# Batch 3's scaled q and k turned by transfers from SP, and joined copies in batch 0, in a gated-attention and mixer kernel

## The chip, the cores and the metric

The kernel runs on one core of a Trainium2 chip. The engines named here are TensorE (PE; its weight loads are listed as PEld), VectorE (DVE), ScalarE (ACT), GpSimd (POOL) and SyncE (SP, which only issues transfers). The metric is the device time of one execution in microseconds, as the median of several runs. A change of less than 1% can't be told from none.

## What is computed

```
f = 1 / (1 + exp(-f_logit))                          # (4, 8, 768, 48): batch, head, step, dim
state = f[t] * state + outer(k[t], v[t])             # per batch and head, 48 x 48
y[t] = q[t] @ state                                  # for 768 steps
x = y, heads side by side                            # (4, 768, 384)
h = relu(x^T @ w_tok1) @ w_tok2                      # mixing over steps, 768 -> 256 -> 768
u = x + h^T
out = u + relu(u @ w_ch1) @ w_ch2                    # mixing over channels, 384 -> 1536 -> 384
```

Inputs and output are float32.

## The kernel before, in words

The 768 steps of a batch are cut into 6 chunks of 128. Within a chunk the recurrence is written as a masked product: ACT makes the log of the gate (`exp`, then `ln`, lines 365 and 366), a cast splits it into a high and a low bf16 part (the low part is `Llo`, line 373), TensorE sums both over the steps with a triangular matrix (`sums`, lines 432 and 433), and ACT takes two exponentials of the sums, `G` and `Gi` (lines 442 and 444). DVE multiplies them onto q and k (`gated`, line 461). These scaled q and k are `qk`, 128 steps by 2 x 8 heads x 64 columns in bf16; 48 of the 64 columns of a head are data.

TensorE needs them with the steps along the columns. In `turn` (line 471) it makes eight transposes of 128 x 128 per chunk into one bank of PSUM, and DVE or ACT copies the bank, 128 x 1024, into `qkT` (`turned`, lines 343 and 345: helpers that serve many copies). Then follow the scores (line 384), the product of the last step's k with v for the state (`parts`, line 400), the mask on DVE (line 512), the new state (lines 520 to 525) and the results (lines 532 and 536). There are two buffers `qkT`, for even and odd chunks, so a chunk's turned q and k can be written when the results of two chunks before are done. From batch 1 on the totals of the gates go through a transfer of 2 KB from SP (`glast`).

Batch 0 goes by pairs of chunks (`pair`, lines 586 to 702): there the two chunks of a pair are dealt out by odd and even steps, so its turned q lies with the columns of both chunks interleaved (`qTp`), and its masks are the constants `pmask`, built by DVE from a triangle (`tri_bf`) and the identity. Turned q and k of each chunk go into banks of their own and are copied one by one (`turned`, four copies of 128 x 512 per pair); the same banks then take the scores.

The mixer of a batch (lines 711 to 809) has two products over the steps (`tok1` line 716, `tok2` line 732), a transpose of the sum (`ut`, line 764, copied into `uT`), and two products over the channels (`ch1` line 780, `ch2` line 798), after which DVE adds the input (line 804) and SP stores 128 rows (line 808).

All four batches overlap: attention of a batch runs between the mixer matmuls of the batch before. The order is not found by the engines but written out by hand in `ORDER`, a list of numbers of operations. Each token is an operation (its place in the order in which the code adds them); a letter behind it picks the engine (A for ACT, D for DVE, G for POOL), a number behind a colon the PSUM bank, and `z3` stands for three filler matmuls on a block of ones (line 826), which write to a bank that is not read. Every engine works through its own operations in the order of this list, SP too: a transfer whose data isn't ready holds back the ones behind it. The loads of q, k, v, gates and weights are issued by POOL, the first gates by SP. The code already holds a path in which a batch named in `TURNED` gets its scaled q and k turned by a transfer; before the change the tuple is empty.

```
if b in TURNED:
    add(("turn", b, c), SP, lambda: nc.sync.dma_start_transpose(
        out=qkT[it], in_=qk[i].rearrange("t n h d -> t (n h d)")), need=[("qh", i), ("kh", i)],
        make=[("qkT", it, 0), ("qkT", it, 1)], kind=("xfer", 1300, 3060))
    return [Bank(), Bank()]
```

Of the kernel before, what the change touches and what calls it, by code (L numbers as in the profile page):

```python
# [22 lines left out]
TURNED = ()  # L23
# [9 lines left out]
41 42 19 8 43 18 27 7 25 5 16 17 26 29 0 6 1 9 44 12 24 61 30 13 32 2 58 46 14 15 10 62 3 31 59 63D 45 64 35 28 33 67  # L33
34 60D 47 65 11 40 70 37 z14 123:0 48 66D 68 73 69D 50 114:1 71 125 72D 162:2 49 116 128 124 118 51 115 39 153:3 36 20
38 74 121:1 117 126 155 75G 127 135:0:4 164 119:5 141 154 131:6 53 157 129:0 120A 146 202:3 132D 130A 143G 167 156 163
52 134 165 122A 166 160:4 138 54 193:2 204 142A 139 161A 133 147 203 137 z1 174:6:0 148G 205 195 168:3 149G 136 194
158:1 76 169A 180 z1 140:5:2 196 159A 181 170:6 197 150 206 171A 172 187 151A 207 z1 173 175 183G 152A 198:0 182G 176
208:2 199A 56 210:1 209A 178 z1 200:4 211A 55 177 201A z3 213 188 77 145A 179:3:6 218 144A 212 217 184 236:5 228:1
185A 215 190G 237 186A 78 214:2 216 189A 238 229 191 220 219:4:3 192A 221 4 223A 222G z1 224 230 80 226 225D 231 239
227A 21 232 240 82 233 241 235D 234A 243A 242D 248:1 244:7 252:2 249 361 260 245 250 261 362 264 246 253 263A 265 363G  # L40
256 254 262A 257 247 266A 272:5 268:4 81 259A 258D 270:0 388:7 273A 269D 278:6 79 271D 391 274:5 279D 276:4 255 292:0
277A 57 267D 300:6 275A 370 294:4 301D 358 326:5 293D 359 302:6 23 371 322:0 327D 303A 324:3 367 360D 316:5 84 295A
251 306:6 389 325D 372G 368 310:1 307D 320:4 311D 83 380:3 308:2 382 87 318:1 383 309D 282:6 390 384 86 321A 284:2 392
381 312:4 369G 323A 385 314:3 285A 393 319A 296:0 91 364 304:2 297D 313A 394:1 305D 373 386:4 395A 283D 286:2 317D
280:0 365 290:5 374 281D 366G 298:6 287A 387D 315A 424:0 375G 22 291A 398:2 299A 396:3 401 397:5 426 409 403G 453:7
427 399 416:6 402G 288:2 428 85 407 418 333:4 419 400 88 456 338:1 408 289A 457 417 404:3 93 420 334 425 421 413:6 90
335 415A 89 405A 422:0 336 343:5 423A 429 92 461:4 406D 430:2 414D 95 462 344 455 431D 463 432:6 410 454 433:3 436
434:4 411A 412A 339 437 94 435 491:6 484:7 345 438 98 445 440A 439A 441:0 444 340 100 442A 458 485 450:2 446 101 464
353:3 452A 341 451A 97 459:4 447 443A 486 492 460A 465:2 448G 99 354 466D 449A 469:0 96 467:1 472 355 470 487 471
468:0 348:4 473 479 474A 475G 493 606 476:1 376 480 609 349 477D 607 494 346 481:0 488 495 482A 483D 350 610 608D 489  # L50
615 496 611G 624:0 490D 497A 328:5 356 612 105 498:6 478D 627 501:3 616 351 628 504:1 626 499 632:7 617G 625 329 505
634 502 510:0 613 506G 513:1 629 503A 500G 507:3 514 633 330 618 508 515G 518:6 635 637 520:4 516:1 614G 630:3 636
521D 517A 511 638:7 342 519A 106 331 668:1 631A 530:6 639D 108 660:0 531A 640:4 661 641:5 509G 644 642:6 663 512G
534:2 662 643 669 550:4 107 652 535A 522:3 538:0 621 523D 103 551A 526:5 524:3 548:2 856 527D 102 525D 532:5 651 857
542:3 670 104 539D 619 528:7 543D 533A 552:0 109 549D 671 540:3 622 620D 672 111 544:2 850 553D 664 572:1 673 851
574:0 645 573A 852G 566:5 665 529A 697:1 545A 646G 536:7 567A 112 700 576:2 537D 647A 701 110 575A 648:5 541D 546:7
332 649A 653 657:3 650D 623G 357 547A 558:6 659D 699 666:0 378 698 654 674:5 658D 655A 667A 554:7 675D 678:3 559A
677:1 681 676:4 656A 555D 858G 853 577 682 865 689 562:7 377 705:6 690 680 560:1 706 556:3 688 563A 581:4 854 702 684A
683G 578 707 855G 582 579 113 868:6 708 583 679 871 869 568:2 872 584 859 685:0 561D 866 585 703:5 870 352 694:7 704D
557A 709:1 696A 691 570:3 569A 710D 693G 695A 713:6 692G 711:2 716 686A 712:4 379 715 735:6 586:7 723 736 876:2 714  # L60
728:1 587 879 687D 860 564:5 724 878 861G 737 877 717 588 571D 718A 719A 720:2 565D 738 873 729 721A 596:3 862 881 730
722A 867D 725:4 597 589 726A 731 874:2 739 732 875A 598 740 727A 733 904:5 734D 741A 882:7 599 912:4 883A 754:1 757:3
755 745:6 907 748:0 758 915 591:1 746 914 759G 916 749 742:3 913 880 751:6 905 743 750G 580 885:0 906 884:4 337 756G
744A 895 886:3 747A 908 592 752 347 888 760:7 753A 601:6 761A 889 593 863 897 909 891A 864G 762:3 890A 764:7 917 602
765A 763D 896 768:4 766:7 792:3 594 767A 603 887 793A 769A 770:1 910:0 604 918:4 898 911A 901:6 900G 941:2 919D 902A
788:3 903A 771D 892:7 921:5 894D 893A 920:6 943 922:1 923 789A 800:7 933 899A 778:0 942 924 816:3 810:5 779D 776:6
801D 782:0 932 774:7 925 783A 946 780:4 777A 811D 772:0 944 781D 812:6 945 773A 926 605 808:2 775A 934 927G 796:0 817A
600 928G 813A 949:7 818:3 950 814:6 819A 802:5 951 806:3 952 784:7 809D 929:1 797D 785A 790:2 931D 815A 938:7 930A
791D 979:6 794:0 798:2 795D 953:1 803D 799A 786:0 939A 954D 947:5 787A 935 972:2 940A 980 948D 840:0 807A 937A 981
936A 957:3 956:7 960 955:4 967 825:3 958 973 820:1 959 982 974 961 835:5 968 962G 964:4 963G 975 826 966A 965A 969:7  # L70
827 970A 976 983 828 830:4 829 977 984 831 978A 985A 804:2 821 805A 832 822 998:2 823 989:6 845:3 990 986:1 999 991A
992:6 987 1000A 841 993 971A 988G 995:1 994A 836 996 1001:6 997G 1008:1 1004:7 1002 1006:2 842 833 1003A 1005D 837
1009A 1007D 846 1012:2 1014:1 847 1013A 1015D 1010:1 1030:7 1011A 1016:4 1031D 1018:6 1017D 1052:7 848 1019A 1044:4
1053D 849 1054:3 1028:7 1055D 1058:1 838 1056:3 1029D 839 1060:5 1059D 1057A 834 1026:7 1061A 590 1040:3 1027D 824
1062:1 1041A 1050:6 1045A 1020:5 1063A 1051D 1042:4 843 1046:6 844 1036:0 1047A 1032:1 1021A 1022:3 1043A 1048:5
1038:4 1094:6 1024:7 1039A 1023A 1079:2 1037A 1089:3 1049A 1033A 1069:4 1025A 1064:0 1034:1 1095 1084:5 1035D 1080
1085 1090 1074:1 1096 1081 1097 1098 1091 595 1086 1070 1087 1065 1082 1092 1075 1093 1071 1088 1076 1083 1072 1066
1073 1077 1078 1067 1068
"""


# [65 lines left out]
def kernel(  # L147
# [147 lines left out]
    for b, c in sorted(TOTALS):  # L295
        memset(f"L{b}{c}", L[b % 2][:, c, :, D:64], 0.0, [("L", b % 2, c)], 200)
# [7 lines left out]
    for i in range(len(state_bd)):  # L304
        memset(f"sbd{i}", state_bd[i], 0.0, [("sbd", i)], 220)
# [553 lines left out]
```

## Time and profile before

| | us |
|---|---|
| median of 3 runs | 177.97 (177.92 to 179.67) |
| the profiled execution | 178.3 |
| its span, first to last instruction | 176.6 |
| TensorE busy | 167.6 (95%) |
| DVE, ACT, POOL busy | 127.9, 120.2, 82.4 |

The profile is of one execution. It lists busy time by engine and the span in 40 slices; windows give the busy time of each engine in a stretch that is chosen (PE, PEld, DVE, ACT, POOL, each with its count, then the granted clock of TensorE, the share of the DMA engines and GB/s). The chain of waits goes back from the last instruction, at each step to what released it, and is shown in order of time (start, length, what). The groups list instructions of one kind with their busy time, the mean in ns of one, and the idle time before them with what ended it. The transfers are listed with their size and the time from issue to landing. Matmuls are pipelined, so the duration listed for one is longer than what it adds to a row of them; a row's length divided by its count gives the latter.

### The profile page before, as it was taken

The numbers are of one execution on the slowest core, as the hardware profiler recorded it, in microseconds if no ns is written. First come the engines' busy times: TensorE is split into PE (matmuls) and PEld (weight loads), VectorE is DVE, ScalarE is ACT, GpSimd is POOL, SyncE is SP. The second block draws the span as 40 slices with busy tenths as digits, with TensorE's granted clock in tenths as the row PEclk, the third lists the DMA queues.
The fourth block names the chain that finished last, engine by engine and source line by source line (L and its number), as shares of the span: only waits on it lengthen the run. The fifth ranks groups of instructions, "written<-read, shape, count | busy, mean of one in ns | idle before, by whom it ended". The sixth has DMA issues, their size and how long they took to land.

```text
span 176.6 us, 4600 instructions
## 1 busy us (share of the span) xinstructions
PE 167.6 (95%) x1835; PEld 107.7 (61%) x1838; DVE 127.9 (72%) x294; ACT 120.2 (68%) x273; POOL 82.4 (47%) x106
## 2 busy tenths in 40 slices
PE   6999898999999999999999999999999999999991
PEld 2466674556676665765757576676676566566660
DVE  6699987986879789897888968989476174830142
ACT  3999967869987569999969679775772444265000
POOL 4977946691799958998993503200001010000000
PEclk9999999999999999999999999999999999999999
DMA  5999999999599998999999991200200100150034
GB/s 149 226 171 184 227 218 206 148 197 156 34 87 138 205 130 179 142 117 91 137 135 149 156 77 47 89 4 0 91 4 0 48 0 0 74 193 4 0 135 176
DMA packets 78500, 19.98 MB, mean 113 GB/s; under 512 B 71216, under 2 KB 77664, under 8 KB 78480
## 3 DMA queue, kind: packets, MB, share of 16 engines
q0 software_dynamic: 69600, 13.77, 89.5%
q1 hardware_dynamic: 8880, 5.93, 11.0%
q8 instruction: 14, 0.23, 0.6%
q14 instruction: 6, 0.05, 0.1%
HBM read 25.17 MB, written 4.72 MB: 169 GB/s over the span
## 4 chain that ended last, share of the span: by engine, by line
PE 65%; DVE 11%; DMA 8%; ACT 7%; POOL 3%; issue 3%; DVEq 0%; POOLq 0%; ACTq 0%
PE ps L780 23%; PE ps L798 19%; DMA f_sb<-in_f_logit_dram 8%; PE ps L732 4%; PE ps L716 3%; PE ps L471 3%; ACT f_sb L365 2%; POOL qk_sb L265 2%; DVE Llo L373 2%; PE ps L764 2%; PE ps L384 1%; PE ps L612 1%; PE ps L433 1%; PE ps L432 1%; PE ps L536 1%
## 5 line engine op out<-in xcount | busy, mean ns | idle before, releaser
L798 PE MATMUL ps<-w_ch,zT 128*128 128x384 bf16 (+2 forms) x300 | 54.9, 320 | 0.0
L780 PE MATMUL ps<-uT,w_ch 128*128 128x384 bf16 x288 | 51.7, 326 | 0.6 <-DVE uT L345 0.3
L780 PEld LDWEIGHTS <-w_ch 128*128 128x128 bf16 x288 | 27.4, 97 | 18.1 <-issue 1.2
L798 PEld LDWEIGHTS <-zT 128*128 128x128 bf16 x300 | 27.4, 97 | 16.6 <-issue 0.4
L351 ACT ACTIVATE zT<-ps 128x384 bf16<-128x384 f32 x56 | 25.1, 496 | 11.2 <-PE ps L780 11.0
L353 DVE TENSOR_SCALAR zT<-ps 128x384 bf16<-128x384 f32 x40 | 20.9, 552 | 12.3 <-PE ps L780 12.2
L512 DVE TENSOR_TENSOR AmT<-ps,tri_bf 128x512 bf16<-128x512 f32 x36 | 23.3, 683 | 0.8 <-PE ps L384 0.7
L804 DVE TENSOR_TENSOR x_nat<-x_nat,ps 128x384 f32<-128x384 f32 (+2 forms) x25 | 13.1, 533 | 13.3 <-PE ps L798 13.1
L347 POOL CAST state_bd<-state 48x192 bf16<-48x192 f32 x20 | 6.9, 347 | 30.0 <-DVE state L525 18.3
L373 POOL TENSOR_TENSOR Llo<-L 128x384 bf16<-128x384 f32 x15 | 13.5, 904 | 12.4 <-ACT L L366 11.0
L265 POOL DMA_DIRECT2D qk_sb<-in_k_dram x16 | 15.9, 995 | 0.1
L265 POOL DMA_DIRECT2D qk_sb<-in_q_dram x16 | 15.9, 993 | 0.0
L265 POOL DMA_DIRECT2D v_sb<-in_v_dram x16 | 15.7, 989 | 0.0
L365 ACT ACTIVATE f_sb<-f_sb 128x384 f32<-128x384 f32 x24 | 12.0, 521 | 3.2 <-DMA f_sb<-in_f_logit_dram 3.1
L461 DVE TENSOR_TENSOR qk<-qk_sb,GG 128x768 bf16<-128x768 bf16 x18 | 10.6, 603 | 4.0 <-ACT GG L444 2.5
L347 POOL CAST u_bf<-x_nat 128x384 bf16<-128x384 f32 x10 | 5.2, 540 | 17.5 <-DVE x_nat L748 17.5
L716 PE MATMUL ps<-x_bf,w_tok 128*128 128x384 bf16 x48 | 12.6, 325 | 0.0
L366 ACT ACTIVATE L<-f_sb 128x384 f32<-128x384 f32 x24 | 12.1, 517 | 0.2
L748 DVE TENSOR_TENSOR x_nat<-x_nat,ps 128x384 f32<-128x384 f32 x21 | 10.8, 548 | 1.3 <-PE ps L732 1.2
L343 ACT ACTIVATE x_bf<-ps 128x384 bf16<-128x384 f32 x20 | 9.7, 493 | 2.4 <-PE ps L702 1.4
L343 ACT ACTIVATE x_nat<-ps 128x384 f32<-128x384 f32 x15 | 7.4, 493 | 4.7 <-PE ps L536 4.5
L471 PE MATMUL ps<-ident,qk 128*128 128x128 bf16 x144 | 10.3, 219 | 0.0
(96 smaller groups left out, 275.8 us busy)
## 6 DMA issues: line engine op xcount, KB each, us to landing
out_dram<-x_nat SPq DMA_DIRECT2D x23, 192.0 KB, 1.9
f_sb<-in_f_logit_dram POOLq DMA_DIRECT2D x3, 1152.0 KB, 10.4
f_sb<-in_f_logit_dram SPq DMA_DIRECT2D x3, 384.0 KB, 4.2
w_ch<-in_moe_w_ch_dram POOLq DMA_DIRECT2D x2, 576.0 KB, 11.1
qk_sb<-in_k_dram POOLq DMA_DIRECT2D x12, 96.0 KB, 7.7
qk_sb<-in_q_dram POOLq DMA_DIRECT2D x12, 96.0 KB, 5.1
v_sb<-in_v_dram POOLq DMA_DIRECT2D x12, 96.0 KB, 6.4
w_ch<-in_moe_w_ch_dram POOLq DMA_DIRECT2D x1, 1152.0 KB, 10.7
```

The lines of the kernel that those rows point to most:

```text
L265: lambda eng=eng, into=into, of=of: eng.dma_start(out=into, in_=of),
L343: nc.scalar.activation(out_, in_, AF.Copy, bias=0.0, scale=1.0)
L351: nc.scalar.activation(out_, in_, AF.Relu, bias=0.0, scale=1.0)
L353: nc.vector.tensor_scalar(out_, in_, 0.0, None, ALU.max)
L365: add(("exp", b, c), ACT, lambda: nc.scalar.activation(fb, fb, AF.Exp, bias=0.0, scale=-1.0), make=[key], kind=el)
L373: op.fn = lambda: (nc.vector if op.engine == DVE else nc.gpsimd).tensor_tensor(lo, full, hi, ALU.subtract)
L471: nc.tensor.transpose(to[:, o + hp, :], blk(src)[:, hp, :], ident)
L512: add(("masked", b, c, p), DVE, lambda half=half, made=made: nc.vector.tensor_tensor(half, made(), tb4, ALU.mult), need=["tri_bf"], make=[ ...
L716: add(("tok1", b, rt, kt), PE, lambda rt=rt, kt=kt, pm=pm: nc.tensor.matmul(banks[pm.at][:, 0:DM], lhsT=w_tok1[:, kt, rt * 128:(rt + 1) * ...
L780: nc.tensor.matmul(banks[pm.at][:, 0:384], lhsT=w[:, kt, c0:c0 + 128], rhs=uT[:, kt, cols], start=(kt == 0), stop=(kt == 2))
L798: nc.tensor.matmul(banks[pm.at][:, 0:n1 - n0], lhsT=zT[:, kt, tt * 128:(tt + 1) * 128], rhs=w_ch2[:, kt, n0:n1], start=(kt == 0), stop=(kt ...
L804: add(("sum", b, tt, n0), DVE, lambda un=un, pm=pm, n=n1 - n0: nc.vector.tensor_tensor(un, un, banks[pm.at][:, 0:n], ALU.add), make=[("x_n ...
```

## The change

Three things are done, and the order is written out anew for all batches.

1. `TURNED` holds batch 3. Its six `turn` operations on TensorE and the six copies behind them are replaced by six transfers from SP, 128 x 1024 bf16 each, from `qk` into `qkT`. The scores of batch 3 get two banks of their own.
2. In batch 0 the transposes of both chunks of a pair write one bank for q and one for k, and one copy of 128 x 1024 each takes them out; the copy of q interleaves the chunks while it reads. The scores get banks of their own and wait for both joined copies.
3. Constants: the extra columns of `L` and `Llo` are cleared for two chunks at a time; the masks `pmask` are made by five instructions in place of eight. The gates of batch 0 are made by `gates_pair`: one `exp` for the two chunks of a pair and, in the second and third pair, one `ln`.

```
-TURNED = ()
+TURNED = (3,)
...
-    for b, c in sorted(TOTALS):
-        memset(f"L{b}{c}", L[b % 2][:, c, :, D:64], 0.0, [("L", b % 2, c)], 200)
+    for m in PAIRS:
+        memset(f"L{m}p", L[0][:, 2 * m:2 * m + 2, :, D:64], 0.0, [("L", 0, 2 * m), ("L", 0, 2 * m + 1)], 200)
+        memset(f"Llo{m}p", Lall[:, 2 * m:2 * m + 2, :, D:64], 0.0, [("Llo", 2 * m), ("Llo", 2 * m + 1)], 110)
...
-            for j in range(2):
-                once(f"pmask{n}{j}", DVE, lambda rows=rows, j=j: nc.vector.tensor_copy(pmask[j][rows, :, 1], tri_bf[rows, rows]),
-                     [("pmask", j)], 110, ["tri_bf"])
-            once(f"pmask{n}2", DVE, lambda rows=rows: nc.vector.tensor_copy(pmask[0][rows, :, 0], tri_bf[rows, rows]),
-                 [("pmask", 0)], 110, ["tri_bf"])
-            once(f"pmask{n}3", DVE, lambda rows=rows: nc.vector.tensor_tensor(
-                pmask[1][rows, :, 0], tri_bf[rows, rows], ident[rows, rows], ALU.subtract), [("pmask", 1)], 110,
-                ["tri_bf", "ident"])
+            once(f"pmask0{n}", DVE, lambda rows=rows: nc.vector.tensor_copy(
+                pmask[0][rows], tri_bf[rows, rows].unsqueeze(2).broadcast_to((64, 64, 2))), [("pmask", 0)], 200, ["tri_bf"])
...
+        once("pmask1", DVE, lambda: nc.vector.tensor_copy(pmask[1], pmask[0]), [("pmask", 1)], 160, [("pmask", 0)])
+        for n, rows in ((0, lo64), (1, hi64)):
+            once(f"pmask1{n}", DVE, lambda rows=rows: nc.vector.tensor_copy(pmask[1][rows, :, 0], exc2[rows, rows]),
+                 [("pmask", 1)], 130, ["exc2"])
...
+    def gates_pair(m):
...
+        add(("exp", 0, c0), ACT, lambda: nc.scalar.activation(fb, fb, AF.Exp, bias=0.0, scale=-1.0), make=keys,
+            kind=("el", 2 * DM, False, 1))
+        if m:
+            logs(c0, 2)
+        else:
+            logs(c0, 1)
+            logs(c0 + 1, 1)
...
-                add(("turn", 0, c, x), PE, lambda n=n, turn=turn: turn(n), need=["ident", (x + "h", j)], bank=p_t[j][n],
-                    kind=mms(*[C] * 4))
-                copies(("turned", 0, c, x), (DVE, ACT), lambda n=n, f=turned_to: f(n), lambda n=n, f=turned_from: f(n),
-                       make=[(x + "Tp", i2, j)], bank=p_t[j][n], kind=("el", 512, True, 2 if n else 1))
+                add(("turn", 0, c0 + j, x), PE, lambda n=n, j=j: turn(n, j), need=["ident", (x + "h", j)], bank=p_t[n],
+                    kind=mms(*[C] * 4))
+            copies(("turned", 0, c0, x), (DVE, ACT),
+                   lambda n=n: kTp[i2].rearrange("p j n t -> p (j n t)") if n else qTp[i2].rearrange("p (x j) -> p x j", j=2),
+                   lambda n=n: banks[p_t[n].at].bitcast(BF16) if n else banks[p_t[n].at].bitcast(BF16).rearrange(
+                       "p (j x) -> p x j", j=2),
+                   make=[(x + "Tp", i2)], bank=p_t[n], kind=("el", 1024, True, 2 if n else 1))
...
-                        nc.tensor.matmul(banks[p_t[j][par].at][64 * k:64 * k + 64, hp * 128:(hp + 1) * 128],
-                                         lhsT=kTp[i2][rows, j, hp, 64 * k:64 * k + 64], rhs=qTp[i2][rows, k, hp, :],
+                        nc.tensor.matmul(banks[p_a[j][par].at][64 * k:64 * k + 64, hp * 128:(hp + 1) * 128],
+                                         lhsT=kTp[i2][rows, j, hp, 64 * k:64 * k + 64], rhs=qT(k, hp)[rows, :],
```

In the new order the transposing transfers of batch 3 stand with chunk 1 first, then 0, 3, 2, 4 and 5; the scores that read them come in the order 1, 0, 3, 2, 5, 4. Five of the six joined copies of batch 0 are on ACT, the k of its first pair is on DVE, and four of its six `Llo` are on DVE where five were. The list holds 27 filler matmuls where the old one held 22. The diff also lets masks of batch 0 be done by POOL (`POOLED`), which stays empty.

## What is predicted

> **What bounds the kernel now.** I read the page's busy line and its slices first, then the windows by stage, then the chain of waits in order of time.
>
> ```profile
> PE 167.6 (95%) x1835; PEld 107.7 (61%) x1838; DVE 127.9 (72%) x294; ACT 120.2 (68%) x273; POOL 82.4 (47%) x106
> PE   6999898999999999999999999999999999999991
> DMA  5999999999599998999999991200200100150034
> 6.00:26.00 20.00, 18.44 (x424) 12.63 (x426) 18.52 (x52) 18.45 (x45) 15.13 (x21) 1.00 1.60 196
> 36.00:100.00 64.00, 63.41 (x687) 41.32 (x685) 54.16 (x111) 53.04 (x121) 51.32 (x59) 1.00 1.62 137
> 100.00:136.00 36.00, 35.48 (x396) 23.91 (x395) 28.70 (x58) 25.13 (x57) 4.37 (x10) 1.00 0.37 44
> 136.00:173.00 37.00, 36.78 (x260) 22.95 (x258) 14.60 (x31) 12.46 (x29) 1.01 (x2) 1.00 0.16 60
> ```
>
> There are two stages with different limits. From 36 us to 173 us TensorE is busy for 63.41 + 35.48 + 36.78 = 135.7 of 137 us at the full granted clock (1.00), so a matmul taken out there shortens the run by its own length, as long as nothing else comes late. From 6 to 26 us batch 0's attention runs, and DVE (18.52 of 20) and ACT (18.45 of 20) are as full as TensorE. There one has to shorten the two of them, or the waits between them. The 40 slices of the DMA row are 4.4 us each; the last full one is the 24th, so the loads are over at about 106 us.
>
> **The turns of batch 3.** In the chain of waits the turning of batch 3's scaled q and k stands with all its six chunks (L471, 8 transposes each):
>
> ```profile
> 103.11 0.45 PE ps L471 x8
> 105.19 0.45 PE ps L471 x8
> 114.77 0.89 PE ps L471 x16
> 129.37 0.45 PE ps L471 x8
> 130.31 0.45 PE ps L471 x8
> 149.35 10.72 PE ps L780 x66
> ```
>
> The sum is 0.45 + 0.45 + 0.89 + 0.45 + 0.45 = 2.69 us of TensorE, all on the path. The change takes them out, so this term is -2.69 us. The six copies out of PSUM behind them go too; they run beside TensorE, and I count nothing for them.
>
> In their place SP issues six transfers that turn 128 x 1024 bf16, 256 KB each. No run shows such a transfer. The nearest rows are SP's stores of 192 KB and its 2 KB transfers of the gate totals, once while the loads run (92 to 97 us) and once after them (107 to 109.5 us), and how long SP itself is held:
>
> ```profile
> out_dram<-x_nat SPq DMA_DIRECT2D x2, 192.0 KB, 5.8
> glast<-grow SPq DMA_DIRECT2D x1, 2.0 KB, 5.8
> out_dram<-x_nat SPq DMA_DIRECT2D x2, 192.0 KB, 2.0
> glast<-grow SPq DMA_DIRECT2D x2, 2.0 KB, 2.0
> 107.61 1.12 SPq L452 DMA_DIRECT2D glast<-grow  x2
> ```
>
> From issue to landing it is 2.0 us on free queues and 5.8 us beside the loads, and the size hardly matters. So the end to take depends on whether loads run beside the transfer. In the new list of orders the last load (v of batch 3) stands some 10 us of matmuls before the first turning transfer; in the old run it landed 8.5 us after its issue:
>
> ```profile
> v_sb<-in_v_dram POOLq DMA_DIRECT2D x1, 576.0 KB, 8.5
> ```
>
> So the first transfer meets a queue that has just become free, and the other five a free one. I take 3 us, near the 2.0 us end with something for the larger size and the turning, and keep 2.0 and 5.8 as bounds.
>
> [...]
>
> Now what hides the 3 us. The reader is the scores op of the chunk, on TensorE in program order. I counted what the new list puts between each transfer and its reader, with these prices beside 10.72 / 22 = 0.49 us for a ch1 group of three matmuls (L780, above):
>
> ```profile
> 163.66 9.13 PE ps L798 x64
> 105.97 1.30 PE ps L732 x8
> 132.13 0.55 PE ps L384 x16
> 74.43 0.36 PE ps L400 x16
> 66.77 0.32 PE ps L433
> 116.85 0.21 PE ps L536 x8
> ```
>
> A ch2 group of four costs 9.13 / 16 = 0.57 on average of two widths (0.65 for a full one, four of the 0.163 us that 1.30 / 8 gives), a tok2 of two 0.33, scores 0.55, parts 0.36 for two chunks and half that for one, a sums op 0.32. Chunk 0 of batch 3 has parts, sums, four tok2, three ch2 and the other chunk's scores between: 0.36 + 0.32 + 1.30 + 1.95 + 0.55 = 4.5 us. Chunk 2 has six ch1, chunk 0's results and the other scores: 2.92 + 0.21 + 0.55 = 3.7 us. Chunk 5 has five ch1, two tok1, a ch2 and parts: 2.44 + 0.33 + 0.65 + 0.18 = 3.6 us. Chunks 1, 3 and 4 have over 5 us. With a landing at L us the stalls are therefore (L - 4.5) + (L - 3.7) + (L - 3.6), each only where positive: nothing at 3 us, and 1.3 + 2.1 + 2.2 = 5.6 us at 5.8 us. I put +0.2 us for a transfer that starts a little late, since SP issues in order: a turn waits for the scaled q and k and for the results of two chunks before, and what stands behind it on SP (gate totals of the next chunks, stores) waits with it. The states that read those totals come several us later, and the stores have time until the end. SP is held 1.12 / 2 = 0.56 us by a transfer today; even at twice that its queue has room, with 15 such issues in the whole stage.
>
> **Batch 0.** Here the rows of the groups by shape and the steps of the chain count:
>
> ```profile
> L343 ACT ACTIVATE zT<-ps 128x512 bf16<-128x512 bf16 x11 | 7.0, 692 | 0.2 <-PE ps L612 0.2
> L345 DVE COPY zT<-ps 128x512 bf16<-128x512 bf16 x1 | 0.4, 411 | 0.0
> L343 ACT ACTIVATE qkT<-ps 128x1024 bf16<-128x1024 bf16 x8 | 8.2, 1021 | 1.5 <-PE ps L471 1.1 <-ACT uT L343 0.4
> L345 DVE COPY qkT<-ps 128x1024 bf16<-128x1024 bf16 x10 | 6.9, 687 | 1.4 <-PE ps L471 1.1 <-PE ps L532 0.3
> L373 DVE TENSOR_TENSOR Llo<-L 128x384 bf16<-128x384 f32 x9 | 5.1, 582 | 1.8 <-ACT L L366 1.8
> L316 DVE COPY pmask<-tri_bf 64x64 bf16<-64x64 bf16 x4 | 1.3, 328 | 0.0
> L320 DVE TENSOR_TENSOR pmask<-tri_bf,ident 64x64 bf16<-64x64 bf16 x2 | 0.4, 224 | 0.0
> L318 DVE COPY pmask<-tri_bf 64x64 bf16<-64x64 bf16 x2 | 0.3, 168 | 0.0
> L323 DVE TENSOR_TENSOR exc<-inc,ident 128x128 bf16<-128x128 bf16 x1 | 0.2, 160 | 0.0
> 7.63 0.66 DVE pmask L316
> 10.38 0.23 DVE pmask L320
> 10.91 0.20 DVE pmask L318
> ```
>
> The twelve copies of turned q and k (11 on ACT, 7.0 us; one on DVE, 0.4 us) become six of double width, five on ACT and one on DVE. A joined copy of k is the shape of the 128x1024 rows: 1.02 on ACT, 0.69 on DVE. A joined copy of q reads PSUM in steps, which no row shows: between 1.02 (the contiguous one) and 2 x 0.69 = 1.38 us (two of today's copies on ACT). ACT then has 2 x 1.02 + 3 x 1.02 to 1.38 = 5.1 to 6.2 us, 0.8 to 1.9 us less, and DVE 0.28 us more. The masks take eight instructions and 2.0 us today (1.3 + 0.4 + 0.3). The new five are two of 64 rows (0.33 each), one of 128 (0.16 by exc, the same size) and two of 64 x 64 (0.17 each): 1.2 us, so DVE saves 0.8. Today 0.66 + 0.23 + 0.20 = 1.1 us of them stand in the chain, so I count 0.5 of the 0.8. One Llo (0.58) moves from DVE to POOL, which has 4.9 of the 20 us free there (15.13 busy). Joined exp and ln and the joined memsets run before or beside that and are counted at nothing. DVE's stretch shrinks by 0.5 + 0.58 - 0.28 = 0.8 us and ACT's by at least as much, so I take -0.8 us for the stage. Against it stands that a joined copy waits for both chunks of the pair; the scores needed q of both before, and only k comes later. As bounds I keep +0.5 us (a gated half of 0.4 to 0.7 us more in the wait) and -1.9 us (all that ACT saves).
>
> The new list also holds 27 filler matmuls where the old held 22, all before the first ch1 group.
>
> ```profile
> 20.34 0.22 PE ps L826
> ```
>
> Five at 0.22 are 1.1 us of TensorE. I cost them at nothing, because TensorE waits there for ACT and DVE (the fillers stand in these waits); if it does not, they take the gain of the stage back.
>
> **The sum.** The profiled execution took 178.3 us (span 176.6 us). 178.3 - 2.69 - 0.8 + 0.2 = 175.0 us. It lies 0.3 us over the median of the runs, 177.97, so I forecast 174.7 us.
>
> **Rivals.** (1) The transfers land late, and the scores wait. The place is TensorE at scores of chunks 0, 2 and 5 of batch 3; the price is 5.6 us at 5.8 us landing, which gives 177.97 - 2.69 - 0.8 + 5.6 = 180.1 us. It decides from 3L - 11.8 = 3.5, so L = 5.1 us; beyond that the change loses. For it speaks that a turning transfer is shown nowhere and that the 2 KB transfer took 5.8 us beside the loads; against it that the loads are done. Chance 0.14.
>
> (2) The transfer is made of eight squares that go one after the other, each like an own issue of 0.56 us with 2.0 us behind the last: 8 x 0.56 + 2.0 = 6.5 us, and SP held 4.5 us, so that the second transfer of a pair starts late as well. The stalls would be 2.0 + 2.8 + 2.9 by the formula and some 2 us in each pair for the second, about 13 us: 177.97 - 3.5 + 13 = 187 us. For it speaks only that eight squares are in it, against it that the size of SP's transfers hardly matters in the rows. [...] Chance 0.06.
>
> (3) The gain goes into new gaps. The order of all instructions is written anew; 137 us of TensorE have only 1.3 us of gaps today, so a new order can hardly have fewer and may have more. Gaps of 1.5 to 5.5 us give 176.2 to 180.2 us, mostly a change that can't be told from none. For it speaks that the list is changed in every batch; against it that the matmuls between are the same ones. Chance 0.21.
>
> (4) Batch 0 gives its whole 1.9 us and the six copies also close the 0.5 us of gaps between 100 and 136 us: 177.97 - 2.69 - 1.9 - 0.5 = 172.9 us or less. Chance 0.04.
>
> The forecast itself has 0.55.
>
> **How the numbers follow.** The forecast's own range is 173.0 (batch 0 at its -1.9) to 176.1 (batch 0 at +0.5 with 0.6 us of stalls or gaps). Up from there the third rival fills 176.2 to 179.5, but for its last 0.03, and about half of the first lies up to 179.5 as well. Outside are (4), (2), half of (1) and the end of (3): 0.04 + 0.06 + 0.07 + 0.03 = 0.20. The range is 173.0 to 179.5. A measurement of this kernel tells 1% from no change, 176.2 to 179.8 us. Faster: the forecast, (4) and a little of (3), 0.60. Same: most of (3) and 0.04 of (1), 0.21. Slower: the rest of (1), (2) and 0.03 of (3), 0.19.
>
> **What would show it.** Right: no L471 of batch 3 in the chain of waits, TensorE's busy time lower by about 2.7 us, the turning transfers landing within 3.6 us, scores of batch 3 (L384's line) with no idle time before them, and the first ch1 group (L780) starting about 0.8 us before today's 32.3 us:
>
> ```profile
> 32.30 3.97 PE L780 MATMUL ps<-uT,w_ch 128*128 128x384 bf16 x23
> ```
>
> Wrong: idle time of TensorE before scores that a DMA ends (rivals 1 and 2), with SP's issues at well over 0.56 us for the second; or idle time spread over other lines (rival 3); or a ch1 start that is not earlier.

## The result and the profile after

| | before | after |
|---|---|---|
| median of the runs, us | 177.96 (177.92 to 179.67) | 175.41 (175.27 to 175.60) |
| ratio to before, 95% interval | | 0.984 [0.982, 0.986] |
| the profiled execution, us | 178.3 | 175.42 |
| its span, us | 176.6 | 173.7 |

The changed kernel is 1.6% faster, 2.55 us by the medians and 2.9 us between the two profiled executions. The busy line of the page and the windows of the first three stages read now:

```profile
PE 165.0 (95%) x1795; PEld 104.5 (60%) x1795; DVE 128.9 (74%) x285; ACT 115.0 (66%) x258; POOL 81.4 (47%) x104
6.00:26.00 20.00, 18.63 (x426) 12.32 (x425) 18.09 (x47) 17.39 (x37) 14.67 (x19) 1.00 1.60 197
36.00:100.00 64.00, 62.83 (x696) 41.43 (x695) 55.80 (x111) 52.78 (x120) 50.85 (x59) 1.00 1.78 142
100.00:136.00 36.00, 35.80 (x366) 22.59 (x364) 26.08 (x54) 23.91 (x58) 3.70 (x8) 1.00 0.46 82
```

TensorE's busy time fell by 2.6 us (167.6 to 165.0; the five more fillers are in the second number). Its idle time, the stretch less the busy time, fell from 0.52 to 0.20 us between 100 and 136 us, where the turns of batch 3 stood, and rose from 0.59 to 1.17 us between 36 and 100 us. Between 26 and 36 us, where the mixer of batch 0 begins, TensorE is busy for 9.35 us in place of 8.91, so its idle time fell from 1.09 to 0.65 us. From 6 to 26 us ACT has 1.06 us less to do (18.45 to 17.39) and DVE 0.43 us less (18.52 to 18.09).

The lines that the prediction named come from four views: the DMA issues (median time from issue to landing), SP's own timeline (start, then the time that SP is held, here for two transfers in a row and for one), the chain of waits, and TensorE's timeline at the first ch1 group.

```profile
qkT<-qk SPq DMA_TRANSPOSE x6, 3.3
```

```profile
104.14 3.42 SPq L498 DMA_TRANSPOSE qkT<-qk  x2
125.89 1.23 SPq L498 DMA_TRANSPOSE qkT<-qk  x1
```

```profile
109.20 0.33 PE ps L408 x8
...
109.53 0.40 PE ps L408 x8
...
118.48 0.49 PE ps L814 x3
118.97 0.55 PE ps L408 x16
...
129.66 0.55 PE ps L408 x16
```

```profile
32.32 0.65 PE L814 MATMUL ps<-uT,w_ch 128*128 128x384 bf16 x3
```

The median transfer lands in 3.3 us; one that stands alone holds SP for 1.23 us. In the chain there is no turn of batch 3 (L495 is the line of the turns now), and the scores of batch 3 (L408) follow the matmuls before them but for one short stop: the second eight in the fence, those of chunk 0, start at 109.53 us, and their weights had waited 0.2 us for the transfer. The first ch1 group (L814) starts at 32.32 us; before the change it was 32.30.

TensorE's waits, by what ended them (us in total, times, longest), hold a long one that was not there before; the timeline shows what ended it:

```profile
PE ps L814 <- DVE x_bf L346: 1.0, 1, 1.0
```

```profile
84.48 0.90 DVE L549 TENSOR_TENSOR state<-tsum,glast 128x192 f32<-128x192 f32 x1
85.31 0.55 DVE L346 CAST x_bf<-ps 128x384 bf16<-128x384 f32 x1
85.90 0.65 PE L814 MATMUL ps<-uT,w_ch 128*128 128x384 bf16 x3 [1.00 <-DVE x_bf L346]
```

A ch1 group wants a PSUM bank that still holds results of batch 2's chunk 0; DVE copies them out as bf16 x only at 85.31 us, behind a state step.

### The profile page after: what moved, and what is told of

Its sections match the earlier page's. It is cut to its first block, busy times and chain, and to the rows that moved or that the text cites. A ratio compares the mean times of both kernels' runs of the same rounds, so it can differ in the third digit from the quotient of the medians.

```text
span 173.7 us, 4503 instructions
## 1 busy us (share of the span) xinstructions
PE 165.0 (95%) x1795; PEld 104.5 (60%) x1795; DVE 128.9 (74%) x285; ACT 115.0 (66%) x258; POOL 81.4 (47%) x104
## 4 chain that ended last, share of the span: by engine, by line
PE 79%; ACT 10%; DVE 5%; DMA 2%; issue 1%; DVEq 0%; ACTq 0%
PE ps L832 26%; PE ps L814 24%; PE ps L750 5%; PE ps L766 4%; PE ps L408 3%; PE ps L798 2%; PE ps L495 2%; DMA f_sb<-in_f_logit_dram 2%; PE ps L863 2%; PE ps L560 2%; PE ps L456 2%; DVE zT L354 2%; PE ps L424 1%; PE ps L556 1%; ACT L L383 1%; ACT f_sb L387 1%
## 5 line engine op out<-in xcount | busy, mean ns | idle before, releaser
L832 PE MATMUL ps<-w_ch,zT 128*128 128x384 bf16 (+2 forms) x300 | 54.3, 319 | 0.0
L814 PE MATMUL ps<-uT,w_ch 128*128 128x384 bf16 x288 | 51.6, 326 | 1.0 <-DVE x_bf L346 1.0
L814 PEld LDWEIGHTS <-w_ch 128*128 128x128 bf16 x288 | 27.3, 98 | 18.3 <-issue 1.5
L352 ACT ACTIVATE zT<-ps 128x384 bf16<-128x384 f32 x56 | 26.0, 498 | 13.7 <-PE ps L814 13.0
L750 PE MATMUL ps<-x_bf,w_tok 128*128 128x384 bf16 x48 | 13.5, 326 | 0.2 <-ACT x_bf L344 0.2
L374 POOL TENSOR_TENSOR Llo<-L 128x384 bf16<-128x384 f32 x13 | 11.0, 848 | 3.0 <-ACT L L367 2.8
L485 DVE TENSOR_TENSOR qk<-qk_sb,GG 128x768 bf16<-128x768 bf16 x18 | 11.5, 644 | 0.9 <-ACT GG L468 0.9
L344 ACT ACTIVATE state_bd<-state 48x192 bf16<-48x192 f32 x22 | 7.9, 360 | 6.2 <-DVE state L549 5.8
L863 PE MATMUL ps<-steady 128*128 128x512 bf16 x27 | 9.8, 476 | 1.5 <-DVE steady L279 1.5
L344 ACT ACTIVATE x_bf<-ps 128x384 bf16<-128x384 f32 x15 | 7.3, 487 | 5.5 <-DVE zT L698 2.0
L766 PE MATMUL ps<-h1T,w_tok 128*128 128x384 bf16 x48 | 10.2, 325 | 0.6 <-ACT h1T L352 0.6
L468 ACT ACTIVATE GG<-ps 128x384 bf16<-128x384 f32 x18 | 8.9, 496 | 0.5 <-PE ps L457 0.5
```

What stands on the lines that cost most here:

```text
L344: nc.scalar.activation(out_, in_, AF.Copy, bias=0.0, scale=1.0)
L352: nc.scalar.activation(out_, in_, AF.Relu, bias=0.0, scale=1.0)
L750: add(("tok1", b, rt, kt), PE, lambda rt=rt, kt=kt, pm=pm: nc.tensor.matmul(banks[pm.at][:, 0:DM], lhsT=w_tok1[:, kt, rt * 128:(rt + 1) * ...
L766: nc.tensor.matmul(banks[pm.at][:, 0:DM], lhsT=w_tok2[:, kt, tt * 128:(tt + 1) * 128], rhs=h1T[:, kt, :], start=(kt == 0 and not held), st ...
L814: nc.tensor.matmul(banks[pm.at][:, 0:384], lhsT=w[:, kt, c0:c0 + 128], rhs=uT[:, kt, cols], start=(kt == 0), stop=(kt == 2))
L832: nc.tensor.matmul(banks[pm.at][:, 0:n1 - n0], lhsT=zT[:, kt, tt * 128:(tt + 1) * 128], rhs=w_ch2[:, kt, n0:n1], start=(kt == 0), stop=(kt ...
```

## The experiments

Each ratio is to the kernel before in runs on the same chip, with its 95% interval; the changed kernel stands at 0.984.

| run | us | ratio |
|---|---|---|
| e1 batch 3 turned by TensorE, new order | 180.55 | 1.013 [1.009, 1.016] |
| e2 old order, transfers at the old turns | 179.01 | 1.005 [1.003, 1.006] |
| e9 old order, transfers behind the gated products | 185.49 | 1.039 [1.037, 1.042] |
| e10 old order, transfers behind the last readers | 177.57 | 0.997 [0.995, 0.998] |
| e4 joined copies of batch 0 split | 176.06 | 0.988 [0.987, 0.990] |
| e3 no fillers inside batch 0 | 176.95 | 0.992 [0.990, 0.995] |
| e8 five fillers less | 175.99 | 0.987 [0.984, 0.991] |
| e11 third pair's exp and ln later | 178.53 | 1.000 [0.997, 1.003] |
| e6 bf16 x of batch 2's chunk 0 earlier | 174.36 | 0.980 [0.977, 0.983] |
| e12 e11 and e6 together | 176.80 | 0.993 [0.991, 0.996] |
| e5 every transfer twice | 186.22 | 1.046 [1.043, 1.048] |
| e7 batch 2 turned by transfers too | 193.24 | 1.076 [1.072, 1.080] |

### What the turning is worth, in the new order and in the old

**e1.** The changed kernel, with TensorE turning batch 3 again and ACT and DVE copying out:

```diff
-TURNED = (3,)
+TURNED = ()
```

> The changed kernel with batch 3's scaled q and k turned by TensorE again (eight transposes a chunk, one copy of 128 x 1024 behind them), all else in the changed order. If the gain is the turning taken off TensorE, this one is slower than the changed kernel by 2.4 to 3.0 us: 177.8 to 178.4 us, level with before. If the gain came from the new order, it stays within 1 us of the changed kernel: below 176.4 us.

It ran at 180.55 us, 5.1 us over the changed kernel by the medians and 4.5 us between the profiled executions (179.88 and 175.42): more than the 2.69 us of the turns. The window of the stage and the wait that stands out in it:

```profile
100.00:136.00 36.00, 34.24 (x364) 22.08 (x363) 25.37 (x53) 24.96 (x56) 3.71 (x8) 1.00 0.15 37
```

```profile
PE ps L815 <- ACT zT L353: 0.9, 1, 0.9
```

TensorE is idle for 1.76 us of the 36, where the changed kernel has 0.20. The turns' 2.69 and this 1.56 make 4.25 of the 4.46 us between the profiles. With the copies out of PSUM back on ACT and DVE, and six more uses of PSUM banks, ch1 has to wait for a bank that ACT empties; the new order, with the turns and copies put in at these places, leaves no room for them.

**e2, e9, e10.** The other way round: the kernel before with its order of all the rest, and the turning of batch 3 alone moved to SP.

```diff
-TURNED = ()
+TURNED = (3,)
...
+    def turned_in(b, c):
+        return 2 if (b, c) == (3, 3) else c % 2
```

The second part of the edit (a third buffer for chunk 3, in the gate buffer of batch 2) is in e9 and e10 only. In e2 each transfer stands where the turn stood:

> The kernel before, in its old order, with only batch 3's turns replaced by transfers from SP (batch 0 and the constants as before). If the turning term is the whole gain: 175.2 to 175.8 us, level with the changed kernel. If the transfers need the new order to be in time, the scores wait and it stays above 176.5 us; TensorE would then show idle time before the scores of batch 3.

That placing lets the transfer of chunk 3 overwrite the turned q that the results of chunk 1 still read, so these are computed with chunk 3's q, and they wait for its transfer:

```profile
PE ps L531 <- DMA qkT<-qk: 1.6, 1, 1.6
```

So its 179.01 us hold a wait that isn't the turning's. e9 was to take it away by issuing earlier:

> The kernel before with its old order and its old batch 0; only the turning of batch 3 goes to SP. Each of the six transfers stands right behind the gated product of its chunk, and chunk 3 has a third buffer for the turned q and k (the gate buffer of batch 2, which nothing reads any more), so that no transfer has to wait for the results of chunk 1. What is computed is the same. If the whole gain of the change is the turning (the term of 2.69 us and the copies), this runs like the changed kernel: ratio to the kernel before 0.981 to 0.987. If the new order and batch 0 carry part of it, this stays at 0.988 to 0.995. If the transfers land after their readers in this order too, TensorE waits before scores for a transfer and the ratio is 1 or more.

It made it worse: chunks 1 and 4 now overwrite the q that the results of batch 2's chunk 5 and of batch 3's chunk 2 read (these two are computed with the later chunk's q), and TensorE stood still for 5.0 us.

```profile
PE ps L536 <- DMA qkT<-qk: 5.0, 1, 5.0
```

```profile
110.00:112.00 2.00, 2.00 (x8) 0.94 (x7) 0.11 (x1) 0.43 (x1) 0.00 (x0) 0.50 0.00 0
112.00:114.00 2.00, 2.00 (x12) 1.14 (x11) 1.58 (x4) 1.51 (x5) 0.00 (x0) 0.83 0.03 8
```

In these windows the column behind the five engines is the granted clock: behind the wait it is 0.50 up to 112 us, 0.83 from 112 to 114 us and 1.00 from 114 to 116. Both kernels tell what a wait costs, not what the turning is worth. e10 puts each transfer behind the last reader of what it overwrites:

> The kernel before with its old order and its old batch 0; only the turning of batch 3 goes to SP, now with every transfer behind the last reader of the turned q and k that it overwrites: chunks 0 and 1 at the place of the old turns, chunks 2, 3 and 5 right behind their gated products, chunk 4 behind the results of chunk 2; chunk 3 again has a third buffer. What is computed is the same. If the whole gain of the change is the turning (the term of 2.69 us and the copies), this runs like the changed kernel: ratio to the kernel before 0.981 to 0.987. If the new order and batch 0 carry part of it, 0.988 to 0.995. If transfers land after their readers in this order too, TensorE waits before scores for a transfer, above all chunk 1 with the shortest cover, and the ratio is 1 or more.

No TensorE wait for a transfer is left, and the gain is 0.6 us (0.997). The stage, and the two longest waits that were shorter before the change:

```profile
100.00:136.00 36.00, 34.42 (x363) 22.02 (x362) 26.39 (x55) 23.08 (x55) 4.16 (x9) 1.00 0.58 86
```

```profile
PE ps L587 <- DVE Llo L377: 1.0, 1, 1.0
PE ps L536 <- DVE x_nat L808: 0.7, 1, 0.7
```

Of the 2.69 us that the turns leave free, 1.06 us went into idle time here (0.52 to 1.58), above all in waits for DVE and ACT to read PSUM banks out; the turns had stood in front of them. The idle time is only a part of it, since a matmul in front of a gap is listed as busy beyond what it adds to a row (e10's page lists the ch1 matmuls with 326 ns each in the mean, and a row of 23 of them takes 3.97 us, 0.17 each). The starts of the same matmuls in both traces tell the whole: the tok1 matmul in front of the first turn starts at 102.79 us before and 102.44 in e10, the ch2 group behind the last one at 130.91 and 129.71. The lead grew from 0.35 to 1.20 us, so 0.85 of the 2.69 us arrived.

Nothing was lost at the start, which the edit doesn't touch. There the sums of batch 0 (L587) wait 1.0 us for a low half of the gate, where the same wait was 0.3 us before the change, but the first ch1 group starts as before the change (32.30 us):

```profile
32.29 3.97 PE L784 MATMUL ps<-uT,w_ch 128*128 128x384 bf16 x23
```

So all three numbers I expected for this run missed the reason: neither a late transfer nor batch 0 keeps the gain down, but the old order. Turning by transfer in place of TensorE is worth 0.6 us in the old order and 5.1 us in the new one, each with one placing of the transfers or of the turns and copies; whether another placing in the old order gives more was not tried.

### Batch 0

**e4.** The joined copies are made as two half copies each, on the same engines at the same place:

```diff
+            def each(eng, out_, in_, n=n):
+                for j in range(2):
+                    copy_on(eng, kTp[i2][:, j].rearrange("p n t -> p (n t)") if n else
+                            qTp[i2].rearrange("p (x j) -> p j x", j=2)[:, j],
+                            banks[p_t[n].at].bitcast(BF16)[:, 512 * j:512 * j + 512])
```

> The changed kernel with each of batch 0's six joined copies done as two copies of 128 x 512, as before. ACT and DVE then have some 2 us more in that stage. If the stage is bound by them, as the prediction took it, it is slower by 0.8 us or more: above 176.2 us. If the joined copies bring nothing because TensorE and its fillers set the stage, it stays within 0.3 us: 175.1 to 175.7 us.

0.988 against 0.984: the split costs 0.65 us by the medians, between the two cases. Not all of it arises in batch 0. In the profiled executions the first ch1 group starts at 32.85 us (32.32 in the changed kernel), and later the scores of batch 3 wait 0.4 us for a transfer, where in the changed kernel only their weights waited, 0.2 us:

```profile
PE ps L408 <- DMA qkT<-qk: 0.4, 1, 0.4
```

So the joined copies are worth about half a microsecond in batch 0. The stepped read of the joined q cost nothing extra here, by the groups by shape of the changed kernel (busy us, then mean ns of one):

```profile
L344 ACT ACTIVATE zT<-ps 128x1024 bf16<-128x1024 bf16 x5 | 4.9, 1014 | 0.1
L344 ACT ACTIVATE qkT<-ps 128x1024 bf16<-128x1024 bf16 x5 | 5.1, 1025 | 2.4 <-PE ps L495 2.4
```

The five of batch 0 (`zT`, three of q and two of k) take 1014 ns in the mean, 1001 to 1024, and the contiguous ones of the later batches 1025.

**e3 and e8.** In e3 the fillers inside batch 0 are left out (14 of 27; the 13 ahead of the first sums stay); in e8 five are (both z3 become z1, and the last z1 goes), which leaves 22 as before the change.

```diff
-... 191A 169 158 z3 155:6:2 ... 159 135A z3 192:4:6 ... 205D 67 z1 206 ...
+... 191A 169 158 z1 155:6:2 ... 159 135A z1 192:4:6 ... 205D 67 206 ...
```

> The changed kernel without the 14 filler matmuls that stand inside batch 0's attention (the 13 ahead of it stay). If the fillers are on the path there, the run is shorter by 0.5 to 1.5 us: 173.9 to 174.9 us, and the first ch1 matmul starts earlier than 32.3 us. If they only fill waits for ACT and DVE, as the prediction took it, it stays at 175.2 to 175.7 us.

> The changed kernel with 22 fillers, as many as before: both groups of three in batch 0's attention cut to one, and the last one taken out. If the five more fillers lie on the path: faster by 0.5 to 1.1 us than the changed kernel, 174.3 to 174.9 us, at a full clock. If the granted clock falls with them, as with all fillers out (0.80 from 20 to 26 us): slower, above 175.8 us. If they only fill waits: 175.2 to 175.7 us.

Neither is faster. e3 is 1.5 us slower than the changed kernel, which none of the theories had expected; its windows of 2 us show why:

```profile
20.00:22.00 2.00, 0.99 (x42) 0.84 (x45) 2.00 (x5) 2.00 (x3) 1.99 (x3) 1.00 0.98 217
22.00:24.00 2.00, 1.30 (x62) 0.98 (x55) 1.82 (x4) 0.57 (x2) 0.00 (x0) 0.91 1.05 218
24.00:26.00 2.00, 2.00 (x25) 1.32 (x18) 1.45 (x5) 1.23 (x3) 0.34 (x1) 0.50 1.13 208
26.00:28.00 2.00, 2.00 (x45) 1.19 (x44) 0.70 (x3) 0.90 (x3) 1.27 (x2) 0.73 1.19 208
```

From 20 to 24 us TensorE is busy for only 2.29 of 4 us, and the clock falls to 0.50 right behind it. As an estimate from the three windows below 1.00, what is lost is 2 x 0.09 + 2 x 0.50 + 2 x 0.27 = 1.7 us of TensorE, about the 1.5 us that e3 is slower. In the changed kernel the clock is 1.00 there. With 22 fillers (e8) the profiled execution keeps 1.00 as well, and the ratios agree within their intervals, so the five more cost nothing that these runs can show: they stand in time in which TensorE waits anyway. They may be of use. Two of e8's six executions had a granted clock of 0.985 and 0.987 over the whole span and took 177.16 and 177.94 us, the other four (0.996 to 0.999) 174.90 to 176.28; the changed kernel had 0.998 to 1.00 in all four of its own. The two also carry the median to 175.99 us, into the range that I had given for a falling clock.

**e11.** In the chain of the changed kernel, ACT's exp and ln of the third pair stand ahead of the gates of the second:

```diff
-... 8 38 11 58 57D 100:1 ... 104 41 59 30 ... 138 60G 111:0 ... 114:5 143 112 61G 140 ...
+... 8 38 11 57D 100:1 ... 104 41 30 ... 138 111:0 ... 114:5 143 58 59 60G 112 61G 140 ...
```

> The changed kernel; of batch 0 the joined exp and ln of the third pair (0.73 and 0.55 us on ACT in the chain) stand behind the gates of chunk 3 instead of ahead of them, and the low half of chunk 4's gate behind that ln. What is computed is the same. If ACT, with the joined exp and ln in front, sets the start of batch 0, the turns of the second pair start 0.5 us earlier and the time falls by 0.3 to 0.6 us (ratio 0.981 to 0.983, with the changed kernel at 0.984). If TensorE, with its fillers, or DVE takes over at once, the time stays within 0.3 us. If the third pair's sums now come late on TensorE, it is up to 0.5 us slower.

The low half of chunk 4 (60) has to move with them, as it reads what that ln writes. e11 took 178.53 us, 3.1 us slower than the changed kernel, with a spread from 176.8 to 179.9. The direction is that of the last case, the size is not, and it has two parts. Four of the twelve executions had a granted clock of 0.997 to 1.00 and took 176.76 to 177.72 us; the other eight had 0.986 to 0.990 and took 178.49 to 179.89. The profiled one is among the four: 177.08 us, 1.7 us over the changed kernel. Its waits:

```profile
PE ps L610 <- POOL Llo L396: 1.0, 2, 0.6
PE ps L657 <- DMA v_sb<-in_v_dram: 0.8, 1, 0.8
```

The third pair's sums (L610) wait for their low halves on POOL, and parts (L657) waits for a load of v. POOL issues the loads too, and a low half that waits there holds them back, as its timeline shows, first of the changed kernel, then of e11:

```profile
10.72 1.63 POOL L396 TENSOR_TENSOR Llo<-L 128x384 bf16<-128x384 f32 x2
12.28 0.92 POOL L264 DMA_DIRECT2D v_sb<-in_v_dram  x1
```

```profile
13.82 1.73 POOL L396 TENSOR_TENSOR Llo<-L 128x384 bf16<-128x384 f32 x2 [3.09 <-ACT L L383]
15.49 0.92 POOL L264 DMA_DIRECT2D v_sb<-in_v_dram  x1
```

Both low halves come 3.1 us later, and the load of v behind them is issued 3.2 us later. What lowers the clock in the other eight executions wasn't profiled. There is no slack of ACT's to be had at this place: the third pair's exp stands early for a reason.

### The new wait, and covers that run out

**e6.** The bf16 copy of x of batch 2's chunk 0 (629 in the list) stands right behind its f32 copy (630), ahead of five other DVE steps that it stood behind:

```diff
-... 651 99 630D 544:5 541D ... 634 681 629D 646:0 ...
+... 651 99 630D 629D 544:5 541D ... 634 681 646:0 ...
```

> The changed kernel with one token moved: DVE's copy of batch 2's chunk 0 into x_bf right behind its copy into x_nat, ahead of the state of chunk 1. In the changed kernel TensorE waits 1.17 us at 84.7 us for the PSUM bank that this copy frees. If this gap is lost time on the path: faster by 0.6 to 1.2 us than the changed kernel, 174.2 to 174.8 us. If another wait takes its place (DVE is full there): within 0.3 us, 175.1 to 175.7 us.

The wait of 1.0 us is gone, the time falls to 174.36 us (0.980), 1.05 us under the changed kernel, and this is the fastest version of the study. The two intervals overlap at their edges, but the traces agree: by the starts of the same matmuls in both, e6 is 0.3 us ahead of the changed kernel at 23 us and 1.3 us ahead at 88 us, behind the place of the wait, so 1.0 us is the edit's. **e12** adds e11's edit to it:

> The changed kernel with the third pair's exp and ln later, as in the run before, and also with batch 2's copy of chunk 0's bf16 x right behind its f32 copy, which took away the gap of 1.2 us at 84.7 us (that edit alone gave 0.980 of the kernel before). What is computed is the same. If both are what they seem, the gains add: 0.977 to 0.980. If the start of batch 0 isn't set by ACT, it is 0.980 again.

It ran at 176.80 us, 1.7 us under e11 and 2.4 us over e6: each edit works in the same direction as alone, in sizes that differ by 0.7 us, which is within the spread of e11. Its scores wait 0.6 us for a transfer, too.

**e5.** Each transfer is issued twice, the first time into a buffer that nothing reads:

```diff
-                out=qkT[it], in_=qk[i].rearrange("t n h d -> t (n h d)")), need=[("qh", i), ("kh", i)],
+                out=to, in_=qk[i].rearrange("t n h d -> t (n h d)")) for to in (spare, qkT[it])], need=[("qh", i), ("kh", i)],
```

> The changed kernel with each of batch 3's turning transfers issued twice in a row, first into a buffer that is not read (a part of batch 2's gates, used up by then), then into its place. SP is held twice 1.24 us and the second lands that much later, so 4.5 us or more after the chunk's first issue in place of 3.3. By the formula of the prediction (cover of 4.5, 3.7 and 3.6 us) the scores then wait 0 + 0.8 + 0.9 us: slower than the changed kernel by 1 to 2.5 us. If the covers are longer than counted: within 0.5 us of it.

10.8 us slower, not 1 to 2.5. SP's timeline, a wait of TensorE and one of SP, and the window of the stage:

```profile
104.17 1.34 SPq L499 DMA_TRANSPOSE f_sb<-qk  x1
105.61 2.34 SPq L499 DMA_TRANSPOSE qkT<-qk  x1
109.12 1.23 SPq L499 DMA_TRANSPOSE f_sb<-qk  x1
110.40 1.32 SPq L499 DMA_TRANSPOSE qkT<-qk  x1
```

```profile
PE ps L409 <- DMA qkT<-qk: 6.7, 3, 3.3
SPq L499 <- DMA f_sb<-qk: 2.3, 3, 1.1
```

```profile
100.00:136.00 36.00, 29.12 (x260) 17.30 (x258) 20.93 (x44) 19.29 (x46) 3.37 (x7) 0.86 0.60 101
```

The second chunk's transfer that counts starts at 110.40 us; in the changed kernel both transfers of the pair are through SP by 107.6 (104.14 + 3.42). The longer hold is not the only reason. All the first transfers go into the same spare buffer, so three of them wait on SP until the one before has landed (2.3 us in all): the first lands at 109.06 us, and the next starts at 109.12. The expectation had left that out, so the run costs more than the hold of SP alone would. TensorE waits 6.7 us, and the clock falls to 0.86 over the stage, which by an estimate is at most another 36 x 0.14 = 5.0 us, since the waits lie in the same 36; the two together are 11.7, against 10.8 measured.

**e7.** Batch 2 is turned by transfers too, while the loads still run:

```diff
-TURNED = (3,)
+TURNED = (2, 3)
```

> The changed kernel with batch 2 turned by transfers too, at the places where TensorE turned it, beside the loads. TensorE loses another 2.69 us of work. If transfers land beside loads in 3.3 us, the scores of chunks 2 to 5 wait some 2.7 us in all, as little is put between there: 175 to 176 us. If they land in 5.8 us or later beside the loads: 180 us or more.

193.24 us, 17.8 us slower than the changed kernel.

```profile
PE ps L408 <- DMA qkT<-qk: 14.0, 4, 7.4
```

```profile
69.28 5.85 SPq L498 DMA_TRANSPOSE qkT<-qk  x2
78.15 13.09 SPq L476 DMA_DIRECT2D glast<-grow  x2
91.34 1.30 SPq L498 DMA_TRANSPOSE qkT<-qk  x1
```

Beside the loads two transfers take SP 5.85 us instead of 3.42; two issues of gate totals, of which one waits for its data, then stand on SP until 91.24 us (78.15 + 13.09), and the next transfer, behind them, starts at 91.34 us. The landing is late as well, up to 9.4 us. The scores wait 14.0 us in all.

## Why the prediction was right, and where it was not

The forecast was 174.7 us, and it became 175.41, faster by more than 1% as forecast. By its terms:

**The turns, -2.69 us: right, but not by themselves.** TensorE's busy time fell by 2.6 us, and between 100 and 136 us no new idle time came up. The premise "as long as nothing else comes late" carried the whole term, though, and I left it untested: with the old order and the placing of e10 the turning gives 0.6 us, since TensorE then runs into copies that come late. That it held is due to the new order of the stage, which the prediction treated as a risk only.

**The six copies "count at nothing": right in the sum.** The stage had 0.52 us of idle time and gave 0.32 of it back. But they are nothing only in an order made for them: put back into the new one they come with 1.56 us of idle TensorE (e1). ACT and DVE have room there (24.96 and 25.37 of 36 us busy in e1), and a bank that was emptied late stopped TensorE all the same, for 0.9 us.

**Landing at 3 us, +0.2 us for late ones: right in the sum, with little to spare.** The median is 3.3 us, and four of the six landed in 3.0 to 3.6. The first two, issued at 104.14 and 105.58 us, took 4.6 and 3.9, past the 3.6 that the prediction had set as a sign. So the weights of chunk 0's scores waited 0.2 us (from the view of `qkT` between 100 and 136 us):

```profile
  PEld L408: 0.2, 1
...
DMA to landing us min/median/max: 3.0/3.3/4.6
```

In e4 and e12, which change nothing at this place, the slower of the two took 4.7 and 4.9 us, and TensorE itself waited 0.4 and 0.6 us. The covers were counted too long: the row of 0.55 us holds 16 matmuls, the scores of two chunks, so the covers of chunks 0 and 2 are 4.2 and 3.4 us. The stores of 192 KB land in 2.0 us (page of the changed kernel) and these 256 KB in 3.3, so the turning transfers took longer here than plain ones, also per byte: 12.9 against 10.4 ns a KB. The hold of SP was too low: 1.23 us, more than the 1.12 I called "twice". My formula for stalls charged nothing for it, and nothing for the clock, so it is too flat: in e5 the clock takes, by the estimate above, up to 5.0 us beside the waits of 6.7.

**Batch 0, -0.8 us: this step failed.** The first ch1 group starts at 32.32 us against 32.30. One pair of executions is a weak measure, as the same batch 0 comes out up to 0.4 us apart. The old batch 0 is in four profiled executions (before, e2, e9, e10), with the start at 32.30, 32.54, 32.54 and 32.29 us, and the new one in four (after, e1, e5, e6), with 32.32, 32.12, 32.37 and 32.00: in the mean 0.2 us earlier, not 0.8. Batch 0's own part didn't get shorter at all: the six tok1 matmuls right behind its last results start at 26.15, 26.33, 26.33 and 26.08 us in the old, and at 26.62, 26.42, 26.67 and 26.30 in the new, 0.3 us later. What was won came behind it, in the idle time between 26 and 36 us.

ACT got the room I counted (1.06 us less to do), DVE half of it (0.43 of 0.8). But the stage was taken as bound by the sum of their work, and by the chain of waits it goes from one engine to the next: in the changed kernel ACT's gate at 11.47 us, DVE's gated product at 11.86, turns on TensorE at 12.63. TensorE's timeline shows where the room went, here the last turns of the third pair and the scores that read them, before and after:

```profile
20.44 0.38 PE L612 MATMUL ps<-ident,qk 128*128 128x128 bf16 x4
...
21.68 0.42 PE L646 MATMUL ps<-zT 48*64 48x128 bf16 x16 [0.21 <-ACT zT L343]
```

```profile
18.41 1.06 PE L636 MATMUL ps<-ident,qk 128*128 128x128 bf16 x12
...
21.83 0.58 PE L668 MATMUL ps<-zT 48*64 48x128 bf16 x26
22.96 0.30 PE L668 MATMUL ps<-zT 48*64 48x128 bf16 x6 [0.55 <-issue]
```

The turns are through 1.3 us earlier (19.47 against 20.82 us), but the first scores that read them start 0.15 us later. ACT has other work until 19.58 us, and then copies from 19.60 to 21.54. The last six scores follow a wait of 0.55 us for which the profile shows no reason; what it is for was not found. It is not the five fillers (e8), and not that ACT's third exp stands too early (e11).

**Five fillers at nothing: right**, as far as e8 shows. What I did not see is that fillers are needed there: without those inside batch 0 the granted clock fell to 0.50 from 24 to 26 us (e3).

**Rivals.** The third, gains that go into new gaps, came true in part: 0.58 us more idle time between 36 and 100 us, with a wait of 1.0 us that e6 removed for 1.05 us. In the two profiled executions the terms are -2.69 for the turns, about 0 for the start of ch1, -0.15 for work that the new order does ahead of it (one pair of sums more, three transposes less), +0.58 from 36 to 100 us and -0.32 from 100 to 136: -2.6 us of the 2.9 between them; 0.3 us stay open. The first rival did not happen, but what it described showed in e7: beside the loads transfers held SP longer (5.85 us for two in place of 3.42), started late (at 91.34 us, behind 13.09 us of other issues), landed in up to 9.4 us, and the scores waited 14.0 us. The second did not happen. The fourth's gaps closed in part (0.32 of 0.52 us), without the gain in batch 0.

## What to carry to other kernels

Work taken off the engine that bounds a kernel is worth its length only if the order behind it fits: turning by transfer gave 0.6 us in one order and 5.1 us in another, so read after such a change which copies or banks TensorE now meets too early. The transposing transfers from SP paid here where the loads were done and the matmuls between issue and reader took about as long as the landing, 3.0 to 4.6 us in the changed kernel and up to 4.9 in e12. In e7, beside the loads, the landing took up to 9.4 us, and two issues ahead of a transfer, one of which waited for its data, held SP for 13.09 us: look at what stands ahead of it on SP. In a stage that goes from engine to engine, an engine's busy time says little about the length of the stage (ACT had 1.06 us less to do in batch 0, and that part got no shorter); follow the chain, and don't take filler matmuls out without looking at the granted clock (0.50 in e3).

## What the runs showed of the hardware

- In e3 the granted clock fell to 0.50 (24 to 26 us) after 4 us in which TensorE was busy for 2.29, with no pause longer than 0.7 us; with 2.90 of the same 4 us (e8's profiled execution) it stayed at 1.00. From 22 us on the windows of 2 us in e3 have 0.91, 0.50 and 0.73, and from 28 us 1.00 again.
- Long waits of TensorE cost more than themselves in two runs: in e9 a wait of 5.0 us was followed by windows at 0.50 up to 112 us, and in e5 the clock took, by the estimate above, up to 5.0 us beside waits of 6.7. The wait of 1.0 us in the changed kernel left it at 1.00 (36 to 100 us).
- ACT read PSUM in steps as fast as in a row (1014 and 1025 ns for 128 x 1024 bf16, changed kernel).
- Two DVE steps took longer beside a POOL step. The state step with 0.90 us above ran beside a POOL subtraction; the same step took 0.36 us where POOL only issued loads (DVE's and POOL's timelines of the changed kernel). Of the twelve such steps only two, with 0.90 and 0.76 us, ran beside a subtraction; the other ten took 0.35 or 0.36. A step of another form (L544, which reads PSUM) took 0.35 us at 76.24 us beside the subtraction at 76.18. That POOL is the cause was not tested. The step of 0.90 us is one of the five steps ahead of the copy that e6 moved:

```profile
60.28 0.36 DVE L549 TENSOR_TENSOR state<-tsum,glast 128x192 f32<-128x192 f32 x1 [0.20 <-DVE tsum L547]
```

```profile
84.30 0.86 POOL L374 TENSOR_TENSOR Llo<-L 128x384 bf16<-128x384 f32 x1
```
